# First-batch rows on two DMA queues, one 32-bit product for every second chunk, other first transfers by GpSimd

## The chip, the cores and the metric

The kernel runs on one NeuronCore of a Trainium2 chip. The metric is the device time of one launch in microseconds, smaller is better. TensorE (PE) multiplies, VectorE (DVE), ScalarE (ACT) and GpSimd (POOL) do the elementwise work, and SyncE (SP) issues DMA transfers; ACT and POOL can issue them too. Instructions of one engine run in the order in which the program lists them; between engines, semaphores make an instruction wait for the data it needs.

## The reference

Eight batches of 2496 rows of 256 numbers go through a Fourier mixing step and then through eight experts, of which each row uses one:

```python
X = np.fft.rfft(x, axis=1)                       # x: (8, 2496, 256)
Yr = X.real @ w_r - X.imag @ w_i + b_r
Yi = X.real @ w_i + X.imag @ w_r + b_i
Y = soft_threshold(Yr, 0.01) + 1j * soft_threshold(Yi, 0.01)
x = np.fft.irfft(Y, n=2496, axis=1).reshape(-1, 256)
e = argmax(x @ w_gate + modality_bias[modality_id])    # one of 8 experts
out = softmax_e * (relu(x @ w1[e]) @ w2[e])            # 256 -> 1024 -> 256
```

## The kernel before

The Fourier transform of length 2496 = 39 x 64 is done in two steps of matrix products. **Step 1** (`s1_*`) sums over 39 positions: rows of a batch lie in three groups of 39 partitions, 22 columns of 64 at a time, and a batch is 11 chunks of 512 numbers per partition. A chunk is split into a rounded high part (`x1h`) and a rest (`x1l`), and three products with the split constant `c_f` (L261 to L263) add up to the 32-bit result; ScalarE evicts it (L266). `s1_split` issues the split and, where rows are not there yet, their load; `s1_chunk` the products, the eviction and, for some chunks, the store to a scratch in DRAM (L277; for batch 0 after chunks 3, 7, 9 and 10, three transfers each, one per partition group).

**Step 2** (`a_load`, `s2_pair`) reads the scratch back in ten slabs of two frequencies (L286), so the first slab needs all stores of its batch, and multiplies by a quarter of table `c_m` in plain 32 bits (L295, one product of 128 columns shows as two instructions). `mix_bias` and `mix_sums` form the complex product with the split weights `wmix` (L332; 24 products of 256 columns for a slab), `shrink` is the threshold, `is2_pair` (L356, table `c_q`) and, at the end of a batch, `pivot` and `is1` are the inverse transform with the gate's product. `Route` then ranks the rows by expert and scatters them with indirect DMAs on GpSimd (L547); the expert stage follows after the eight batches.

The order on PE, ACT, DVE and POOL is the order of the program text (`manual_schedule`). `tc.issue_after(ins)` only keeps the transfers of its block behind `ins` on the same issuing queue. `build` writes the start out by hand (L1045 to L1088): constants and the rows of batch 0, eleven chunks of batch 0 with transfers of batch 1's rows and of table `m` between the stores, the mixing weights, the first slabs, then six chunks of batch 1 among the slab products `s2(0)`, `s2(1)`, the mixing `mix(0)` and its bias. The loop over batches and slabs (L1092 on) does for slab p of batch b: load slab p+4, product of slab p+2, chunks of batch 1 (while b is 0), mixing of slab p+1, inverse step of slab p. All plain transfers are issued by SP; GpSimd issues the scatters alone.

Each transfer has one of eight semaphores in turn; an issue waits until the transfer eight places before has landed.

Of the kernel before, what the change touches and what calls it, by code (L numbers as in the profile page):

```python
# [54 lines left out]
def shape_constants(nb):  # L55
# [39 lines left out]
    c_f = hl(cols(blk_f), 1).reshape(P1, 256)  # L95
    c_g = hl(cols(blk_g), 1).reshape(PK, 256)
# [12 lines left out]
    for c in range(2):  # L109
# [13 lines left out]
        "c_m": c_m, "c_q": c_q, "c_f": c_f, "c_g": c_g,  # L123
# [4 lines left out]
class Attn:  # L128
# [24 lines left out]
    def consts_first(self):  # L153

        nc, I, cp = self.nc, self.I, self.cp
        self.m = cp.tile([128, K1 * 128], F32, name="c_m")
        self.q = cp.tile([128, K1 * 128], F32, name="c_q")
        self.f = cp.tile([P1, 2, 128], F32R, name="c_f")
        st = self.w1.tile([128, 2, 256], F32, tag="u", name="st_f")[:P1].rearrange("p a b -> p (a b)")[:, :256]
        nc.sync.dma_start(st, I["c_f"])  # L160
        nc.vector.tensor_copy(self.f, st.rearrange("p (h k) -> p h k", h=2))
# [8 lines left out]
    def table_load(self, t, k):  # L170

        o = slice(k * 512, (k + 1) * 512)
        return self.nc.sync.dma_start((self.m if t == "m" else self.q)[:, o], self.I["c_" + t][:, o])

    def consts_mix(self):
        nc, I, cp = self.nc, self.I, self.cp
        st = []
        for i, nm in enumerate(("w_r", "w_i")):
            st.append(self.ww.tile([128, 520], F32, tag="wr", name=f"st_w{i}")[:, :512].rearrange("p (c d) -> p c d", c=2))
            nc.sync.dma_start(st[i], I[nm].rearrange("(c p) d -> p c d", p=128))  # L180
        for i, nm in enumerate(("b_r", "b_i")):
            nc.sync.dma_start(self.bias[64 * i:64 * i + 64, :],
# [28 lines left out]
    def s1_load(self, b, u, end=None, eng=None):  # L211
# [15 lines left out]
        for g in range(3):  # L227
            ins = eng.dma_start(xt[g * N1:(g + 1) * N1, :n, :], xv[:, GB[g] + 4 * u:GB[g] + 4 * u + n, :])
# [4 lines left out]
    def s1_split(self, b, c):  # L233
        nc = self.nc
        u, h = c // 2, c % 2
        for v in (u, u + 1):
# [5 lines left out]
        (nc.vector.tensor_copy if b == 1 or b == 0 and c % 2 == 0 else nc.scalar.copy)(xh, x)  # L242
# [3 lines left out]
    def s1_chunk(self, b, c, ahead):  # L246
# [3 lines left out]
        xh, xl = self.xs.pop((b, c))  # L250
# [10 lines left out]
        nc.tensor.matmul(ps[:PK], self.f[:, 0, :PK], xh, start=True, stop=False)  # L261
        nc.tensor.matmul(ps[:PK], self.f[:, 1, :PK], xh, start=False, stop=False)
        nc.tensor.matmul(ps[:PK], self.f[:, 0, :PK], xl, start=False, stop=True)  # L263
# [9 lines left out]
        if beg is not None:  # L273
            o = 0 if b == 0 else 4 * u
            for g in range(3):
                lo, hi = beg + (2 if g == 2 and beg == 0 else 0), 2 * c + 2
                self.stored = nc.sync.dma_start(  # L277
                    self.scr[b][:, GB[g] + lo:GB[g] + hi, :],
                    src[g * 2 * K1:(g + 1) * 2 * K1, lo - o:hi - o, :])

# [719 lines left out]
def build(tc, I, out, nb):  # L1000
    nc = tc.nc
    with ExitStack() as outer:
        dp = outer.enter_context(tc.tile_pool(name="wsp", bufs=1, space=DRAM))
        wsp = dp.tile([E * 128, 8192], F32, name="wsp")
        with ExitStack() as ctx:
# [40 lines left out]
            for u, v in ((0, 1), (1, 3), (3, 5)):  # L1046
                at.s1_load(0, u, v)
            first = at.s1_load(0, 5)
            at.s1_split(0, 0)
            at.s1_split(0, 1)  # L1050
            mixing = at.consts_mix()
            for c in range(11):
                at.s1_chunk(0, c, 2)
                with tc.issue_after(at.stored.ins if c > 2 else first.ins):
                    if c == 3:
                        at.table_load("m", 0)
                    elif c == 7:
                        at.s1_load(1, 0)
                    elif c == 9:
                        ins = at.s1_load(1, 1, 3)  # L1060
            with tc.issue_after(at.stored.ins):
                next(mixing, None)
                for i in range(3):
                    ins = load(i)
                    if i < 2:
                        with tc.issue_after(ins.ins):
                            ins = at.s1_load(1, 3, 5) if i else at.table_load("q", 0)
            with tc.issue_after(ins.ins):
                at.table_load("m", 1)
                rt.load_ids(0)  # L1070
            ahead1 = 6 if nb > 1 else 0
            at.s1_split(1, 0)
            at.s1_split(1, 1)
            for c in range(ahead1):
                with tc.issue_after(ins.ins):
                    at.s1_chunk(1, c, 2)
                if c == 1:
# [150 lines left out]
```

## Time and profile before

| | us |
|---|---|
| median of three runs | 1543.49 (1543.16 to 1543.94) |
| profiled execution | 1546.72 |
| its span, first to last instruction | 1544.9 |
| PE busy | 1497.0 (97%) |
| VectorE / ScalarE / GpSimd busy | 710.1 / 660.0 / 512.8 |

The profile is of one execution. PE runs are pipelined, so their ends are modelled. The granted clock of TensorE has two levels, 1.2 GHz (shown as 0.50) and 2.4 GHz (1.00).

### The profile page before, as it was taken

Reading aid. Unit: us, or ns where it says so; the run is one execution under the profiler, and the core shown is the slowest. Engines: PE = TensorE matmul, PEld = TensorE weight load, DVE = VectorE, ACT = ScalarE, POOL = GpSimd, SP = SyncE. Lnnn points to the kernel's source line nnn. Section 1 sums busy time; section 2 is a strip of 40 time slices with the busy share of each in tenths; the row PEclk is TensorE's granted clock in tenths of the full one; section 3 lists DMA queues with packets and bytes.
Section 4 is the critical chain, followed back from the end, with each engine's and each line's share of the span. In section 5 each row is a group of like instructions: output and inputs, shape, how many; then the busy total and the mean of one; then the engine's idle time right before and its main releaser. Section 6 shows DMA issues by size and latency. Waiting matters only on the chain. (4 is left out here: it accounts for less than half of the span.)

```text
span 1544.9 us, 35019 instructions
## 1 busy us (share of the span) xinstructions
PE 1497.0 (97%) x12459; PEld 1465.4 (95%) x12459; DVE 710.1 (46%) x1497; ACT 660.0 (43%) x1345; POOL 512.8 (33%) x511
## 2 busy tenths in 40 slices
PE   4899999999999999999999999999999999999998
PEld 2899999999999989999999999999999998999998
DVE  3676666666666665444333333333333333333332
ACT  2466766676757554523232332332323222233232
POOL 0001444444444545325532232322322323223232
PEclk8899999999999999999999999999999999999999
DMA  7857786868686666523443324552225238626440
GB/s 196 247 179 261 222 269 212 277 212 277 205 261 190 207 196 236 172 44 84 110 91 80 118 55 151 163 157 43 52 47 155 53 68 306 197 40 205 111 151 33
DMA packets 289589, 244.44 MB, mean 158 GB/s; under 512 B 208448, under 2 KB 243852, under 8 KB 285161
## 3 DMA queue, kind: packets, MB, share of 16 engines
q1 hardware_dynamic: 270421, 200.60, 44.9%
q0 software_dynamic: 18992, 41.58, 8.2%
q8 instruction: 100, 1.64, 0.5%
q14 instruction: 76, 0.62, 0.1%
HBM read 432.70 MB, written 100.08 MB: 345 GB/s over the span
## 5 line engine op out<-in xcount | busy, mean ns | idle before, releaser
L849 PE MATMUL y<-w,hh 128*128 128x256 f32 x2496 | 434.6, 278 | 0.2 <-DMA w<-wsp 0.2
L819 PE MATMUL h<-xh,w 128*128 128x256 f32 x2496 | 403.8, 278 | 4.1 <-DMA w<-wsp 4.1
L849 PEld LDWEIGHTS y<-w,hh 128*128 128x128 f32 x2496 | 377.8, 188 | 1.0 <-ACT xh L798 0.3
L849 PE MATMUL y<-w,hl 128*128 128x256 f32 x1248 | 347.2, 278 | 0.3 <-DVE hl L822 0.2
L819 PEld LDWEIGHTS h<-xh,w 128*128 128x128 f32 x2496 | 339.9, 189 | 4.5 <-issue 3.9
L822 DVE SCALAR_TENSOR_TENSOR hl<-h,hh 128x512 fp32r<-128x512 f32 x312 | 209.4, 689 | 232.2 <-ACT hh L821 188.5
L862 POOL DMA_INDIRECT out<-o,ix x161 | 158.5, 984 | 427.0 <-ACT o L841 389.7
L819 PE MATMUL h<-xl,w 128*128 128x256 f32 x1248 | 245.5, 278 | 0.0
L821 ACT ACTIVATE hh<-h 128x512 fp32r<-128x512 f32 x312 | 178.2, 595 | 155.7 <-PE h L819 137.0
L849 PEld LDWEIGHTS y<-w,hl 128*128 128x128 f32 x1248 | 234.3, 188 | 1.3 <-DVE hl L822 0.9
L819 PEld LDWEIGHTS h<-xl,w 128*128 128x128 f32 x1248 | 189.6, 189 | 0.0
L841 ACT ACTIVATE o<-y,xt 128x256 f32<-128x256 f32 x78 | 37.0, 475 | 343.0 <-PE y L849 343.0
L839 DVE TENSOR_SCALAR o<-y,xt 128x256 f32<-128x256 f32 x78 | 37.7, 484 | 314.2 <-ACT o L841 310.1
L332 PE MATMUL mx<-wmix,Xh 128*128 128x256 f32 x1280 | 180.7, 284 | 0.9 <-ACT mx L312 0.6
L799 POOL TENSOR_TENSOR xl<-tr,xh 128x512 fp32r<-128x512 f32 x78 | 101.0, 1295 | 192.9 <-ACT xh L798 192.9
L332 PEld LDWEIGHTS mx<-wmix,Xh 128*128 128x128 f32 x1280 | 160.6, 189 | 3.1 <-ACT mx L312 2.7
L547 POOL DMA_INDIRECT xs<-x1b,si x88 | 88.0, 1000 | 85.2 <-ACT ph L377 33.4
L372 PE MATMUL pv<-pv,z 128*120 128x136 f32 x704 | 111.0, 283 | 0.5 <-ACT z L359 0.5
L547 POOL DMA_INDIRECT xs<-x,si x88 | 87.9, 998 | 71.2 <-ACT ph L377 32.4
L994 POOL TENSOR_TENSOR wl<-wr,wh 128x512 fp32r<-128x512 f32 x46 | 58.5, 1273 | 148.2 <-ACT wh L993 133.7
L378 DVE TENSOR_TENSOR pl<-pv,ph 120x264 fp32r<-120x264 f32 x176 | 75.9, 431 | 68.4 <-ACT ph L377 58.2
L372 PEld LDWEIGHTS pv<-pv,z 128*120 128x120 f32 x704 | 99.5, 186 | 6.7 <-ACT z L359 0.7
(186 smaller groups left out, 1998.4 us busy)
## 6 DMA issues: line engine op xcount, KB each, us to landing
w<-wsp SPq DMA_DIRECT2D x166, 2048.0 KB
a<-scr SPq DMA_DIRECT2D x80, 256.0 KB
xt<-xs SPq DMA_DIRECT2D x624, 32.0 KB
wr<-in_moe_w SPq DMA_DIRECT2D x64, 256.0 KB
wsp<-wh SPq DMA_DIRECT2D x64, 256.0 KB
wsp<-wl SPq DMA_DIRECT2D x64, 256.0 KB
scr<-ev SPq DMA_DIRECT2D x98, 160.0 KB
x<-in_x SPq DMA_DIRECT2D x96, 156.0 KB
```

The costliest lines, as they stand in the source:

```text
L332: self.nc.tensor.matmul(ps[i][:, i, :], t[:, 2 * i + c, o:o + 128], self.w[:, wi, c, lo, :], start=False, stop=n == len(ops) - 1, skip_gro ...
L372: nc.tensor.matmul(ps[:PK, c * 128:c * 128 + D // 2 + E], self.z[:, o:o + 3, :, :].rearrange("p n k r -> p (n k r)"), self.pv[:, c, :], st ...
L378: nc.vector.tensor_sub(pl, ps[:PK, :GC], ph)
L547: i = self.nc.gpsimd.indirect_dma_start(out=self.xs, out_offset=bass.IndirectOffsetOnAxis(ap=si[:, k:k + 1], axis=0), in_=rows, in_offset= ...
L799: nc.gpsimd.tensor_sub(xl, tr, xh)
L819: nc.tensor.matmul(ps[:, q, :], w1[:, lo, c, f * 128:(f + 1) * 128], x[:, c, :], start=n == 0, stop=n == 5)
L821: nc.scalar.activation(hh[:, 2 * p:2 * p + 2, :], ps, AF.Relu)
L822: nc.vector.scalar_tensor_tensor(hl[:, 2 * p:2 * p + 2, :], ps, 0.0, hh[:, 2 * p:2 * p + 2, :], ALU.max, ALU.subtract)
L839: nc.vector.tensor_scalar_mul(o[:, s, :], y[s], gate)
L849: nc.tensor.matmul(y[s], lhsT, w2[:, lo, f, :], start=n == 0, stop=n == 23)
L862: ins = self.nc.gpsimd.indirect_dma_start(out=self.out, out_offset=bass.IndirectOffsetOnAxis(ap=ix, axis=0), in_=o, in_offset=None, bounds ...
L994: eng.tensor_sub(lo, raw, hi)
```

## The change

Rows of batch 0 for the third partition group are issued by ScalarE, those of the first two by SP. In batch 0 the even chunks are no longer split: one product of the plain 32-bit rows with the unrounded constant `c_f1` takes the place of three. The odd chunks are split on VectorE alone. Eight products of a zero tile in bf16 come first on PE and fourteen more after chunk 10. Of batch 0's stores the third group's goes by GpSimd, as do the mixing weights and biases (the generator `consts_mix` is first stepped after chunk 7, which issues its loads), batch 1's rows, most tables, and batch 2's rows. Four slabs are asked for directly behind the stores. Two chunks of batch 1 instead of six stand ahead of the loop, behind `s2(0)`, `s2(1)` and `mix(0)`; the rest follow two per slab. The routing constants and ids move to later slabs of batch 0.

```diff
 def consts_first(self):
+    self.blank = cp.tile([128, 512], BF16, name="blank")
+    nc.vector.memset(self.blank, 0.0)
+    self.f1 = cp.tile([P1, 128], F32, name="c_f1")
+    nc.sync.dma_start(self.f1, I["c_f1"])
...
+def consts_split(self):
+    st = ...
+    nc.scalar.dma_start(st, I["c_f"])
+    nc.vector.tensor_copy(self.f, st.rearrange("p (h k) -> p h k", h=2))
+
+def warm(self, n):
+    ps = self.ps.tile([128, 512], F32, tag="z", name=f"warm_{n}")
+    for _ in range(n):
+        self.nc.tensor.matmul(ps, self.blank[:, :128], self.blank, start=True, stop=True)
...
 # s1_load
         for g in range(3):
+            if b == 0:
+                eng = nc.scalar if g == 2 else nc.sync
...
 # s1_split
+        if b == 0 and h == 0:
+            return
...
-        (nc.vector.tensor_copy if b == 1 or b == 0 and c % 2 == 0 else nc.scalar.copy)(xh, x)
+        (nc.vector.tensor_copy if b < 2 else nc.scalar.copy)(xh, x)
...
 # s1_chunk
+        if b == 0 and h == 0:
+            nc.tensor.matmul(ps[:PK], self.f1[:, :PK], self.xt[b, u][:, :2, :].rearrange("p j d -> p (j d)"),
+                             start=True, stop=True)
+        else: (the three split products)
...
-                self.stored = nc.sync.dma_start(
+                ins = (nc.gpsimd if b == 0 and g == 2 else nc.sync).dma_start(
...
 # build, the start
             at.consts_first()
-            for u, v in ((0, 1), (1, 3), (3, 5)):
+            at.s1_load(0, 0)
+            at.consts_split()
+            for u, v in ((1, 3), (3, 5), (5, 6)):
                 at.s1_load(0, u, v)
-            first = at.s1_load(0, 5)
-            at.s1_split(0, 0)
+            ins = at.table_load("m", 0)
+            at.warm(8)
             at.s1_split(0, 1)
-            mixing = at.consts_mix()
+            mixing = at.consts_mix(nc.gpsimd)
             for c in range(11):
                 at.s1_chunk(0, c, 2)
-                (c == 3: table_load("m", 0); c == 7: s1_load(1, 0); c == 9: s1_load(1, 1, 3))
+                if c == 7:
+                    next(mixing, None)
             with tc.issue_after(at.stored.ins):
-                (mixing loads; load(0), table q, load(1), s1_load(1, 3, 5), load(2), table m, ids)
+                load(0)
+                ins = load(1)
             with tc.issue_after(ins.ins):
+                load(2)
+                ins = load(3)
+            for u, v in ((0, 1), (1, 2), (2, 3), (3, 5), (5, 6)):
+                at.s1_load(1, u, v, nc.gpsimd)
+                if u in (0, 2):
+                    at.table_load("q" if u == 0 else "m", u // 2, nc.gpsimd)
+            at.warm(14)
+            next(mixing, None)
+            s2(0)
+            bias(0)
+            s2(1)
             at.s1_split(1, 0)
             at.s1_split(1, 1)
+            mix(0)
+            bias(1)
+            ahead1 = 2
             for c in range(ahead1):
-                (six chunks, with s2(0), bias(0), s2(1), mix(0) between)
+                at.s1_chunk(1, c, 2)
...
 # build, slab p of batch 0
-                                    at.table_load("m", p // 2 + 2)
-                                at.table_load("q", p // 2 + 1)
+                                at.table_load("m", p // 2 + 2, nc.gpsimd)
+                            at.table_load("q", p // 2 + 1, nc.gpsimd)
...
-                        if p == 3:
+                        if p == 6:
                             late = [rt.consts(), at.consts_last()]
-                        if p in (3, 6):
+                        if p in (6, 8):
...
-                            at.s1_load(b + 2, (1, 2, 3, 5, 7, 9).index(p))
+                            at.s1_load(b + 2, (1, 2, 3, 5, 7, 9).index(p), None, None if b else nc.gpsimd)
```

## Rows read from the trace of the kernel before

**Rows 1.** Page of the profile, its first line and the first line of part 1: span; then for each engine busy us, share of the span and instructions (PE is TensorE's matmul, PEld its weight load, DVE VectorE, ACT ScalarE, POOL GpSimd).

```profile
span 1544.9 us, 35019 instructions
...
PE 1497.0 (97%) x12459; PEld 1465.4 (95%) x12459; DVE 710.1 (46%) x1497; ACT 660.0 (43%) x1345; POOL 512.8 (33%) x511
```

**Rows 2.** Windows of the execution. Columns: window, its length, then busy us (and instructions) of PE, PEld, DVE, ACT and POOL, the granted TensorE clock (1.00 is 2.4 GHz; before the first recorded change at 27 us the column shows 1.00 whatever the clock was), the mean busy share of the 16 DMA engines, and GB/s moved.

```profile
0.00:15.00 15.00, 5.41 (x12) 3.20 (x13) 4.85 (x10) 4.25 (x7) 0.19 (x4) 1.00 0.73 167
...
0.00:39.00 39.00, 15.70 (x39) 8.83 (x39) 12.60 (x25) 11.50 (x19) 0.19 (x4) 0.85 0.73 196
60.00:1540.00 1480.00, 1463.95 (x12317) 1441.08 (x12315) 682.98 (x1446) 639.86 (x1309) 512.51 (x507) 1.00 0.53 157
...
9.00:12.00 3.00, 0.60 (x2) 0.00 (x0) 0.00 (x0) 0.00 (x0) 0.00 (x0) 1.00 0.78 147
...
27.00:30.00 3.00, 0.00 (x0) 0.00 (x0) 0.00 (x0) 0.00 (x0) 0.00 (x0) 0.52 0.59 202
...
45.00:48.00 3.00, 2.99 (x12) 2.47 (x10) 2.48 (x6) 1.87 (x4) 0.00 (x0) 0.56 0.91 195
48.00:51.00 3.00, 2.24 (x15) 1.84 (x16) 2.93 (x6) 0.59 (x1) 0.00 (x0) 1.00 0.78 249
...
57.00:60.00 3.00, 3.00 (x30) 3.00 (x29) 2.44 (x6) 1.36 (x3) 0.00 (x0) 1.00 1.03 347
```

**Rows 3.** Waits of PE, longest in total first: before 50 us (first two rows) and from 60 us to the end (third row). Columns: who, line, released by whom, us in total, times, longest.

```profile
PE s L261 <- DVE x1h L242: 18.9, 4, 8.5
PE s L295 <- DMA a<-scr: 7.6, 1, 7.6
...
PE h L819 <- DMA w<-wsp: 4.1, 2, 3.7
```

**Rows 4.** Timeline of PE. Columns: start us, us, engine, line, operation, tiles and shapes, count merged into the row; in brackets the idle time before it and what ended it.

```profile
6.51 0.78 PE L261 MATMUL s<-x1h,c_f 117*120 117x512 f32 x1 [6.51 <-DVE x1h L242]
...
22.40 0.49 PE L263 MATMUL s<-x1l,c_f 117*120 117x512 f32 x1
...
41.89 2.05 PE L295 MATMUL s<-c_m,a 128*128 128x128 f32 x8 [7.57 <-DMA a<-scr]
...
46.29 1.69 PE L295 MATMUL s<-c_m,a 128*128 128x128 f32 x8
48.76 0.47 PE L261 MATMUL s<-x1h,c_f 117*120 117x512 f32 x1 [0.77 <-DVE x1h L242]
...
49.73 1.08 PE L332 MATMUL mx<-wmix,Xh 128*128 128x256 f32 x8
...
52.46 0.40 PE L261 MATMUL s<-x1h,c_f 117*120 117x512 f32 x1
...
53.18 1.06 PE L295 MATMUL s<-c_m,a 128*128 128x128 f32 x8
...
59.20 1.06 PE L295 MATMUL s<-c_m,a 128*128 128x128 f32 x8
60.01 0.48 PE L261 MATMUL s<-x1h,c_f 117*120 117x512 f32 x1
```

**Rows 5.** Timeline of SP's DMA queue: start of the issue, us the issue took (several merged where xN), line, tile written and tensor read.

```profile
0.74 0.47 SPq L160 DMA_DIRECT2D st_f<-in_c_f  x1
1.27 7.15 SPq L228 DMA_DIRECT2D x<-in_x  x12
...
23.08 4.35 SPq L228 DMA_DIRECT2D x<-in_x  x3
...
29.17 1.95 SPq L228 DMA_DIRECT2D x<-in_x  x3
31.23 1.04 SPq L277 DMA_DIRECT2D scr<-x1b  x3
...
39.02 0.37 SPq L286 DMA_DIRECT2D a<-scr  x1
```

**Rows 6.** Timeline of GpSimd (POOL) in the first batch's scatter: indirect transfers of 117 rows each.

```profile
177.98 0.99 POOL L547 DMA_INDIRECT xs<-x1b,si  x1 [1.38 <-ACT ph L377]
179.28 0.99 POOL L547 DMA_INDIRECT xs<-x1b,si  x1 [0.30 <-issue]
180.57 0.99 POOL L547 DMA_INDIRECT xs<-x1b,si  x1 [0.30 <-issue]
```

**Rows 7.** Timeline of VectorE and ScalarE: the first constant's use, the split of chunk 6 of batch 0, an eviction, and the split of batch 0's first slab product (which goes on with the half-size steps up to 45.73).

```profile
3.00 0.29 DVE L161 CAST c_f<-st_f 117x256 fp32r<-117x256 f32 x1 [3.00 <-DMA st_f<-in_c_f]
...
17.57 0.43 DVE L242 CAST x1h<-x 117x512 fp32r<-117x512 f32 x1 [1.40 <-PE s L262]
18.06 0.58 ACT L266 COPY x1b<-s 120x512 f32<-120x512 f32 x1
...
43.97 0.58 ACT L300 CAST Xh<-s 128x512 fp32r<-128x512 f32 x1 [9.03 <-PE s L295]
...
44.59 0.69 DVE L301 TENSOR_TENSOR Xl<-s,Xh 128x512 fp32r<-128x512 f32 x1 [3.77 <-ACT Xh L300]
45.73 0.42 DVE L303 TENSOR_TENSOR Xl<-Xh,s 128x256 fp32r<-128x256 f32 x1 [0.45 <-ACT Xh L302]
```

More of the change, by code (lines that the diff above doesn't have):

```diff
@@ L95, in shape_constants @@
     c_f = hl(cols(blk_f), 1).reshape(P1, 256)
+    c_f1 = np.ascontiguousarray(cols(blk_f), np.float32)
     c_g = hl(cols(blk_g), 1).reshape(PK, 256)
@@ L122, in shape_constants @@
         "c_tri": tri, "c_grid": grid(seg), "c_grid2": grid(seg, seg, np.zeros((3, 1)), half),
-        "c_m": c_m, "c_q": c_q, "c_f": c_f, "c_g": c_g,
+        "c_m": c_m, "c_q": c_q, "c_f": c_f, "c_f1": c_f1, "c_g": c_g,
         "c_tok": np.concatenate([tok, valid], 1),
@@ L260, in s1_chunk @@
         ps = pool.tile([128, 512], F32, tag=tag, name=f"s1_{b}_{c}")
[L261 to L263 removed]
+        if b == 0 and h == 0:
+            nc.tensor.matmul(ps[:PK], self.f1[:, :PK], self.xt[b, u][:, :2, :].rearrange("p j d -> p (j d)"),
+                             start=True, stop=True)
+        else:
+            xh, xl = self.xs.pop((b, c))
+            nc.tensor.matmul(ps[:PK], self.f[:, 0, :PK], xh, start=True, stop=False)
+            nc.tensor.matmul(ps[:PK], self.f[:, 1, :PK], xh, start=False, stop=False)
+            nc.tensor.matmul(ps[:PK], self.f[:, 0, :PK], xl, start=False, stop=True)
         if ahead and c + ahead < 11:
@@ L1053, in build @@
                 at.s1_chunk(0, c, 2)
[L1054 to L1060, printed above, removed]
-            with tc.issue_after(at.stored.ins):
[L1062 to L1067, printed above, removed]
@@ L1072, in build @@
+            at.warm(14)
[3 more added lines that the diff above has]
+            s2(1)
             at.s1_split(1, 0)
             at.s1_split(1, 1)
+            mix(0)
+            bias(1)
+            ahead1 = 2
             for c in range(ahead1):
-                with tc.issue_after(ins.ins):
-                    at.s1_chunk(1, c, 2)
-                if c == 1:
-                    s2(0)
-                    next(mixing, None)
-                    bias(0)
-                if c == 3:
-                    s2(1)
@@ L1083, in build @@
-                if c == 4:
-                    mix(0)
-            bias(1)
-            ins = load(3)
-            with tc.issue_after(ins.ins):
-                at.s1_load(1, 5)
+                at.s1_chunk(1, c, 2)
             state = None
@@ L1107, in build @@
                         if p == 9:
-                            sw.load()
-                            sw.load()
-                        if p == 3:
+                            with tc.issue_after(ins.ins):
+                                sw.load()
+                                sw.load()
+                        if p == 6:
                             late = [rt.consts(), at.consts_last()]
-                        if p in (3, 6):
+                        if p in (6, 8):
                             with tc.issue_after(ins.ins):
@@ L1120, in build @@
                         ahead(i)
-                    if p == 1 and b > 0:
-                        rt.load_ids(b)
+                    if p == 1:
+                        with tc.issue_after(ins.ins):
+                            rt.load_ids(b)
                     if p in (1, 2, 3, 5, 7, 9) and b + 2 < nb:
                         with tc.issue_after(ins.ins):
-                            at.s1_load(b + 2, (1, 2, 3, 5, 7, 9).index(p))
+                            at.s1_load(b + 2, (1, 2, 3, 5, 7, 9).index(p), None, None if b else nc.gpsimd)
                     if b > 0 and p < (7 if b < 5 else 6):
```

24 lines of the change are left out of this document (10 added, 14 removed).

## The prediction

> **What bounds the kernel now.** I read the page first: TensorE (PE) is busy 97% of 1544.9 us, the next engine 46% [rows 1]. So only two things can shorten the program: less PE work, or less time in which PE has nothing to do. The windows say where PE is idle: 1463.95 of the 1480 us from 60 to 1540 are busy, but 15.70 of the first 39 [rows 2]. The waits agree: 27 us before 50 us are waits for first-batch rows and for the first slab of the scratch, and after 60 us the longest single wait is 3.7 us [rows 3]. From the mixing product at 49.73 on PE runs practically without a gap, so what the change does to that point it does to the end, one for one.
>
> What sets 49.73 is read from the PE timeline and SP's queue side by side. Chunk 6 of batch 0 can start only at 17.57, when its rows are split [rows 7]; the eleven chunks end at 22.40 + 0.49 [rows 4]. Their results go to the scratch, but SP puts six transfers of batch 1's rows (1.4 MB) between the stores: issues at 23.08 and 29.17, the last stores at 31.23, and the first slab is asked for only at 39.02, when all stores have landed [rows 5]. It is there at 41.89 [rows 4]. PE has then been idle for 19 us, save two chunks of batch 1, and runs at the lower of its two clock levels: the granted clock is 0.52 in 27 to 30 and 0.56 in 45 to 48, so it fell at about 27.1 (4.2 us after the last product) and rose at about 47.6, 5.7 us after work resumed [rows 2, 4].
>
> **The change part by part.** Everything before the first mixing product is re-laid; I follow the chain to it.
>
> *Rows of batch 0.* 2.57 MB go as before, a third of them now by ScalarE's queue, plus 0.06 MB for c_f1. Later end: the rate does not move, chunk 6 starts 0.06 MB / 0.167 MB per us = 0.4 us later, 17.9. Earlier end: the 2.34 MB of rows that chunk 6 needs, with 0.18 MB of constants, move at the 0.347 MB per us of 57 to 60 instead of the 0.167 of the first 15 us [rows 2]: 7.3 us from 2, so 9.3. I take 15.5, nearer to the row of the same transfers, yet below it, because 0.147 in 9 to 12, with nothing but these rows under way [rows 2], is less than half of what the same queue moves later.
>
> The Trainium skill speaks against this step. "DMA: Bandwidth & Descriptors", section "Issuing engines are not separate DMA queues", says that transfers of all issuing engines run on the same 16 DMA engines, and that a second issuer saves issue time only. SP's twelve issues took 7.15 us from 1.27, long before 17.57 [rows 5, 7], so by that rule nothing is saved here; that is a rival below.
>
> *32-bit products.* The six even chunks lose a cast and a subtraction on VectorE and three products, and get one 32-bit product. A product of four slabs, 4 x 128 columns in 32 bits, takes 0.81 us (59.20 to 60.01); three split products of 512 columns take 0.72 (52.46 to 53.18) [rows 4]. So PE pays 0.1 us more per even chunk at full clock (6 x 0.1), all inside its idle time; if the clock is low, 1.7 [rows 4] for 0.81. In exchange chunks 6 and 7 need 0.81 + 0.72 + an eviction of 0.58 [rows 7] and some 0.4 of hand-over: chunk 7 is out at 15.5 + 2.5 = 18.0; call it T. At low clock T is 1.5 later.
>
> *Zero products.* 8 before the first rows, 14 after chunk 10. PE waits there anyway (until 6.51 [rows 4] and, from 20, for the slab), so their 3 us each cost nothing. The first eight may make the chunks run at full clock. The fourteen end near 24; the slab comes more than 4.2 us later by the sum below, so I let the clock fall as it did at 27.1 and count no gain; if the cover were gone, 14 products cost 14 x 0.24 = 3.4 us.
>
> *Transfers by GpSimd.* Its queue gets, in this order from T: a third of the store of chunks 4 to 7, the four of the mixing weights and biases (they are asked for at chunk 7, not at the start), the thirds of the last two stores, then fifteen of batch 1's rows with two tables between them. The trace has no plain transfer on this queue. Below: SP's 0.37 us per issue (39.02). Above: an indirect one occupies it 0.99 us and follows the last by 1.29 us [rows 5, 6]. I take P = 1.1, nearest to GpSimd's own row, since most have 39 or 40 rows instead of 117. So the last store is written out at T + 7P = 25.7 and landed 2.3 us later (the first constant, 0.74 to 3.00 [rows 5, 7]): the slab is asked for at 28.0 instead of 39.02. Check by bytes: constants 0.18, rows 2.57, table 0.26, stores 2.56, weights and biases 0.65 = 6.2 MB must move before; from 1.5 on that ends at 19.4 by the rate of 57 to 60 and at 33.2 by the 0.196 of the first 39 us [rows 2]. 28.0 lies between; both ends are kept.
>
> *From the slab to the mixing product.* Arrival 2.9 us after the request (39.02 to 41.89): 30.9. Two slab products at low clock, 1.7 each [rows 4], then the split of the first, 43.97 to 46.15 on ScalarE and VectorE, begins 0.5 after its products [rows 7]: 30.9 + 1.7 + 0.5 + 2.2 = 35.3 for the mixing product, against 49.73. The clock rises 5.7 us after 30.9, at 36.6, so 1.3 us of the mixing run at half speed and lose 0.7. Five chunks of batch 1 that PE had done by 49.73 are now still to do: 5 x 0.72 = 3.6. Shift: 35.3 + 0.7 + 3.6 - 49.73 = -10.1.
>
> *What is late next.* The third slab product needs the second quarter of table m, eleventh on GpSimd's queue after the stores: T + 18P + 2.3 = 40.1; PE is there at 35.3 + 0.7 + 2.7 + 1.4 = 40.1. No cover is left, so I charge one wait of the size of 48.76's, 0.77 [rows 4]: -9.4. Constants and ids moved to later steps of batch 0, its later tables and batch 2's rows on GpSimd: used 9 us or more after issue, since a step of that loop takes 6 us (53.18 to 59.20 [rows 4]); PE covers them, and I cost them at nothing; if one is late, it costs a wait like the 3.7 of [rows 3].
>
> *Sum.* The profiled execution took 1546.7 us around a span of 1544.9; minus 9.4 gives 1537.3 around 1535.5. The timed runs' median, 1543.5, lies 3.2 below that execution: 1534.1, say 1534.0.
>
> **The rivals.**
> 1. *The second queue brings the rows nothing.* Chunk 6 at 17.9, T and all behind it 2.4 later: 1536.4. For it: SP's issues are far ahead of use. Against: the low rate while only rows move.
> 2. *Bytes bind, not issue.* The store lands at 33.2 by the old mean rate: 5.2 later, 1539.2. For it: less than 28 us for 6.2 MB needs a rate that only later windows show.
> 3. *Both relieved.* Rows at the 0.249 MB per us of 48 to 51 [rows 2], so chunk 6 at 12.1 and T at 14.6, GpSimd's issue near SP's 0.37, and all 6.2 MB at 0.28, between 0.249 and 0.347: stores landed at 23.6 instead of 28.0, so 4.4 earlier throughout: 1529.6. For it: nothing holds a queue of its own but bytes. Against: no row shows two queues at once.
> 4. *Slower: GpSimd's issue becomes the bound.* It must write seventeen transfers before batch 1's rows and both tables are out, which SP did at 0.4 us each. The third slab product stood at 53.18 before; with four more chunks to do behind it, 4 x 0.72, it may come at 50.3 for no change. T + 18P + 2.3 reaches that at P = 1.67; at P = 2.0 it is 56.3 and the time 1549.5. Between 1.5 and 1.83 nothing is to be measured. For it: 128 rows of a table or 256 of a weight may take longer than 117 of a scatter. Against: the scatter's 1.29 holds the reading of its indices too. For it also speaks the same page, section "SWDGE vs HWDGE vs iDMA": GpSimd writes its descriptors into SBUF, from which VectorE locks it out in some modes. The scatters' 0.99 us stand beside a VectorE 46% busy [rows 1, 6], so the trace shows no such loss.
>
> **How the numbers follow.** Forecast 0.41, rival 1 0.20, rival 2 0.13, rival 3 0.11, no measurable change (P 1.5 to 1.83) 0.08, slower 0.07. A measurement tells 0.2%, 3.1 us, from no change. Faster: 0.41 + 0.20 + 0.13 + 0.11 = 0.85; same 0.08; slower 0.07. The forecast's own range, P from 0.9 to 1.3 and T from 16.5 to 19.5, is 1531 to 1538. The range for 8 in 10 reaches to rival 3 and past rival 2: 1528 to 1540.5.
>
> **What would show it.** Right: the request for the first slab near 28, the first mixing product near 35, PE without gaps from there, and GpSimd's transfers about 1.1 us apart. Chunk 6 starting at 17 to 18 speaks for rival 1; GpSimd idle while the stores land late, for rival 2; that request before 25, for rival 3; PE waiting for table m or rows of batch 1 after 38, for rival 4. The prediction is wrong if the first mixing product comes after 46, or if it comes early and PE loses it again before 100 us.

## The result, and the profile after

The changed kernel takes 1554.86 us (median of six runs, 1552.54 to 1561.44), the kernel before 1543.33 us in the same session (1542.34 to 1544.77). The ratio is 1.0083, interval 1.0060 to 1.0107: slower by 0.8%, where 9.4 us less were forecast. The profiled execution took 1556.07 us around a span of 1554.3, 9.4 us more than the span before. The medians lie 11.5 us apart; what follows takes apart the 9.4 of the two profiled executions. First the page: span, engines and DMA queues (packets, MB, share of 16 engines' span).

```profile
span 1554.3 us, 35059 instructions
...
PE 1503.1 (97%) x12475; PEld 1466.2 (94%) x12475; DVE 706.3 (45%) x1491; ACT 657.3 (42%) x1340; POOL 540.4 (35%) x561
...
q1 hardware_dynamic: 266453, 190.55, 42.3%
q0 software_dynamic: 22192, 50.69, 10.3%
...
q10 hardware_dynamic: 338, 1.00, 0.3%
```

PE has 6.1 us more busy time than in [rows 1]. GpSimd has 50 instructions more, all of them plain transfers; q0 is its queue, q10 ScalarE's and q1 SP's. The windows, with the columns of [rows 2]:

```profile
0.00:33.00 33.00, 20.66 (x49) 8.88 (x49) 7.46 (x16) 7.72 (x12) 6.82 (x16) 0.96 0.72 193
0.00:39.00 39.00, 20.66 (x49) 8.88 (x49) 8.17 (x17) 7.72 (x12) 11.75 (x25) 0.89 0.74 202
39.00:60.00 21.00, 13.09 (x67) 11.58 (x68) 7.76 (x15) 5.72 (x12) 7.43 (x15) 0.64 0.96 245
60.00:1540.00 1480.00, 1464.62 (x12321) 1441.21 (x12320) 689.24 (x1459) 643.43 (x1316) 519.23 (x520) 1.00 0.53 156
```

From 60 us on PE is as busy as before (1464.62 of 1480 us, 1463.95 in [rows 2]), so the loss lies ahead of 60 us or behind the last product. PE's waits up to 90 us name the place:

```profile
PE s L317 <- DMA a<-scr: 19.4, 2, 15.6
```

The wait for the slabs of the scratch has grown from 7.6 us [rows 3] to 19.4. The timeline of PE:

```profile
1.19 3.59 PE L180 MATMUL warm<-blank 128*128 128x512 bf16 x8 [1.19 <-DVE nlam L167]
7.29 2.03 PE L277 MATMUL s<-x,c_f 117*120 117x512 f32 x2 [2.51 <-DMA x<-in_x]
...
13.74 2.06 PE L277 MATMUL s<-x,c_f 117*120 117x512 f32 x2 [3.13 <-DMA x<-in_x]
...
19.85 1.02 PE L277 MATMUL s<-x,c_f 117*120 117x512 f32 x2
...
43.06 2.05 PE L317 MATMUL s<-c_m,a 128*128 128x128 f32 x8 [15.57 <-DMA a<-scr]
48.96 2.07 PE L317 MATMUL s<-c_m,a 128*128 128x128 f32 x8 [3.85 <-DMA a<-scr]
50.68 2.05 PE L354 MATMUL mx<-wmix,Xh 128*128 128x256 f32 x8
...
55.04 0.40 PE L281 MATMUL s<-x1h,c_f 117*120 117x512 f32 x1
...
56.45 1.05 PE L317 MATMUL s<-c_m,a 128*128 128x128 f32 x8
```

s2(0) starts 1.2 us later than before (41.89 in [rows 4]), although the chunks are through at about 24.4 and the zero products at 27.5. s2(1), which had its slab in time before, waits another 3.9 us. The first mixing product comes at 50.68 instead of 49.73. The mixing takes 4.36 us to the chunk at 55.04 (2.73 from 49.73 to 52.46 in [rows 4]), as its first products still run at the lower clock level: 1.63 more. Then there are five chunks of batch 1 to do that had been done, 5 x 0.72 = 3.6. Sum: 0.95 + 1.63 + 3.6 = 6.2 us. Product for product, PE is 6.3 us late at 78 us and 6.4 us late at the end.

Why the slabs are late is read from SP's queue and GpSimd's, side by side. SP's:

```profile
1.25 9.44 SPq L242 DMA_DIRECT2D x<-in_x  x8
...
17.72 13.09 SPq L297 DMA_DIRECT2D scr<-x1b  x8
36.28 15.14 SPq L308 DMA_DIRECT2D a<-scr  x6
```

GpSimd's:

```profile
22.58 0.55 POOL L297 DMA_DIRECT2D scr<-x1b  x1 [3.78 <-ACT x1b L286]
23.11 0.78 POOL L192 DMA_DIRECT2D st_w<-in_w_r  x1
...
25.67 1.08 POOL L297 DMA_DIRECT2D scr<-x1b  x2
26.69 0.55 POOL L242 DMA_DIRECT2D x<-in_x  x1
29.84 0.52 POOL L242 DMA_DIRECT2D x<-in_x  x1 [2.59 <-DMA scr<-x1b]
...
32.85 0.56 POOL L185 DMA_DIRECT2D c_q<-in_c_q  x1 [0.59 <-DMA st_w<-in_w_i]
33.41 2.50 POOL L242 DMA_DIRECT2D x<-in_x  x5
```

SP has its last store of batch 0 written out at 30.81 (17.72 + 13.09), GpSimd its last at 26.75 (25.67 + 1.08). Yet the first slab is asked for at 36.28: the last stores took 5.5 us from there to land. In the meantime GpSimd had gone on at once to what stood next in its queue, batch 1's rows and the tables; nothing holds these back but its own eight places (one of the rows waited 2.59 us for a store of GpSimd's, at 29.84). How much of the DMA engines each queue had is shown by the queues in the window from 24 to 48 us, of the changed kernel:

```profile
q0 software_dynamic: 1360, 4.15, 63.4%
q1 hardware_dynamic: 1123, 1.72, 25.7%
```

and of the kernel before:

```profile
q1 hardware_dynamic: 2387, 5.35, 79.3%
```

SP's queue, with two thirds of the stores and all slabs, was left with a quarter of the DMA engines' time; GpSimd's had 63%, most of it for rows and tables that nobody needed before 50 us.

The remaining 3 us are behind the last product. The start of the last scatter, in the changed kernel and in the kernel before:

```profile
1545.50 0.97 POOL L884 DMA_INDIRECT out<-o,ix  x1 [1.76 <-DVE o L861]
```

```profile
1539.14 0.97 POOL L862 DMA_INDIRECT out<-o,ix  x1 [1.76 <-DVE o L839]
```

From there to the end of the span are 8.8 us (1554.3 - 1545.50) against 5.8 (1544.9 - 1539.14). Most of that time is GpSimd's closing drain instruction, 5.71 us against 3.26 in the trace's records, which is 2.45 of the 3.0; it also starts 0.6 us later behind the scatter. 6.4 + 3.0 = 9.4 us of span.

### The profile page after: what moved, and what is told of

It reads as the page before. It is cut to its first block, busy times and chain, and to the rows that moved or that the text cites. A ratio compares the mean times of both kernels' runs of the same rounds, so it can differ in the third digit from the quotient of the medians.

```text
span 1554.3 us, 35059 instructions
## 1 busy us (share of the span) xinstructions
PE 1503.1 (97%) x12475; PEld 1466.2 (94%) x12475; DVE 706.3 (45%) x1491; ACT 657.3 (42%) x1340; POOL 540.4 (35%) x561
## 3 DMA queue, kind: packets, MB, share of 16 engines
q0 software_dynamic: 22192, 50.69, 10.3%
## 5 line engine op out<-in xcount | busy, mean ns | idle before, releaser
L569 POOL DMA_INDIRECT xs<-x1b,si x88 | 88.0, 1000 | 84.5 <-ACT ph L399 35.3
```

The lines of the kernel that those rows point to most:

```text
L569: i = self.nc.gpsimd.indirect_dma_start(out=self.xs, out_offset=bass.IndirectOffsetOnAxis(ap=si[:, k:k + 1], axis=0), in_=rows, in_offset= ...
```

## The experiments

The theory: what GpSimd issues, held back by nothing, shares the DMA engines with batch 0's last stores and the first slabs. The rivals: bytes at a fixed rate bind, whoever issues them; the weights, asked for at chunk 7, are what stands in the way; GpSimd's plain transfers cost at the end of the program alone; the zero products matter. Experiments go by their labels, e1 to e16. The first four stand beside a kernel before of 1544.38 us.

**Batch 1's rows back on SP, behind the four slabs.**

```diff
-            for u, v in ((0, 1), (1, 2), (2, 3), (3, 5), (5, 6)):
-                at.s1_load(1, u, v, nc.gpsimd)   # and tables q0, m1 by nc.gpsimd
+            with tc.issue_after(ins.ins):
+                for u, v in ((0, 1), (1, 2), (2, 3), (3, 5), (5, 6)):
+                    at.s1_load(1, u, v)          # and the tables, on SP
```

> Batch 1's rows and the two tables among them go back to SP's queue, behind the four slabs; all else as in the changed kernel. Theory 'turns' (slab reads lose because GpSimd's queue has large transfers under way on the same DMA engines): the stores stop competing with batch 1's rows, the first slab is asked for at 32 to 34 instead of 36.3, arrives about 3 us later instead of 6.6, slabs 1 to 3 follow about 1 us apart instead of 4 to 6, the first mixing product comes at 39 to 42 instead of 50.7, and the time falls by 6 to 11 us against the changed kernel. Rival 'bytes' (the same bytes must move, whoever issues them): the slabs come early but PE then waits for batch 1's rows or table m, which now stand behind them, and the time stays within 3 us of the changed kernel.

Measured (e1): 1552.87 us, ratio 1.0065 (1.0041 to 1.0089). The slabs did land close together, so that s2(0) and s2(1) ran back to back, but the request was no earlier (37.13). Its GpSimd timeline shows what took their place: the rows gone, GpSimd ran ahead to what came next in its queue, the tables of the loop (26.03, 28.48) and batch 2's rows (from 30.84). The time stayed within 3 us of the changed kernel's, as the rival had it; that the request would be no earlier was expected by neither. Taking away one load put another in its place, so e1 alone could not tell the theory from bytes.

**The weights asked for at the start, no zero products, and batch 2's rows on GpSimd in the kernel before.**

```diff
             mixing = at.consts_mix(nc.gpsimd)
+            next(mixing, None)
             for c in range(11):
                 at.s1_chunk(0, c, 2)
-                if c == 7:
-                    next(mixing, None)
```

> The mixing weights and biases are asked for at the start, not after chunk 7. If the stores land late because these 0.65 MB stand among them on GpSimd's queue and on the engines, the first slab is asked for some 3 us earlier (0.65 MB at the 0.21 MB per us of that stretch), and the time falls by about 3 us. Rival: at the start they delay the rows of batch 0 by as much, chunk 7 comes 2 to 3 us later, and the time stays within 1 us.

Measured (e2): 1559.2 us, ratio 1.0096 (1.0076 to 1.0116). The request moved from 36.28 to 39.17 and s2(0) from 43.06 to 51.20. 0.65 MB put ahead of the stores made the request 2.9 us later; at the 0.2 MB per us of the first 39 us they take 3.2. So asking early gains nothing; that it costs this much neither side had expected.

```diff
-            at.warm(8)
-            at.warm(14)
```

> The changed kernel without its 8 + 14 zero products. If they do nothing: clock up at about 20 us as before, the first slab asked for within 0.5 us of 36.3, time within 1 us. If the eight warm the clock for the first chunks: chunks 2 to 5 later, clock up 2 to 4 us later, time 1 to 3 us longer. If the fourteen cost PE: time shorter by up to 3 us.

Measured (e4): 1555.66 us, ratio 1.0061 (1.0042 to 1.0080); request at 34.96, s2(0) at 42.89, mixing at 51.21. The interval overlaps with the changed kernel's: the zero products cost or gain nothing that can be told here.

```diff
-                            at.s1_load(b + 2, (1, 2, 3, 5, 7, 9).index(p))
+                            at.s1_load(b + 2, (1, 2, 3, 5, 7, 9).index(p), None, None if b else nc.gpsimd)
```

> The kernel before, with batch 2's rows (18 transfers) alone issued by GpSimd. Theory 'drain' (the more plain transfers GpSimd has issued, the longer it drains at the very end): the start up to 60 us is as before, GpSimd's last drain is longer than the 3.3 us of before, 4.2 if in proportion to the number of transfers or 5.7 if any suffice, and the time is 1 to 3 us over the kernel before. Rival (the drain's length has to do with the last outputs): the drain is 3 to 3.6 us and the time that of the kernel before within 1 us.

Measured (e3): 1551.43 us, ratio 1.0042 (1.0028 to 1.0056), 7 us over the kernel before where 1 to 3 were expected. This edit of the kernel before was meant to touch the end alone, and touched the start. GpSimd's timeline:

```profile
1.30 1.83 POOL L228 DMA_DIRECT2D x<-in_x  x3 [0.86 <-POOLq L1218]
```

Batch 2's first rows, which stand in slab 1 of the loop, go out at 1.30 us, beside batch 0's: the first chunk starts at 8.97 instead of 6.51 [rows 4], and s2(0) 3.0 us later. At the end, the last scatter to the end of the span takes 6.8 us instead of 5.8. One edit, two costs: a transfer that runs ahead, and a longer end.

**What is left when GpSimd has no plain transfers behind its stores, or none.** The next four stand beside a kernel before of 1544.35 us.

```diff
# the first run's edit, and in the loop
-                            (tables and batch 2's rows) ..., nc.gpsimd)
+                            with tc.issue_after(ins.ins): (the same on SP)
```

> The changed kernel, but GpSimd keeps only the third group's four stores and the weights and biases; batch 1's rows and the first tables are asked for by SP behind the four slabs, the loop's tables and batch 2's rows by SP as in the kernel before. The theory (transfers that GpSimd issues with nothing to hold them back share the DMA engines with the last stores and the first slabs) expects the first slab to be asked for at 31 to 33 us instead of 36 to 37, to land 3 to 4 us later, the first mixing product at 37 to 40 us instead of 50.7, GpSimd's last drain near 3.5 us instead of 5.7, and a time of 1534 to 1541 us. The rival (the bytes of the start bind, whoever issues them) expects the request at 35 us or later, mixing at 46 us or later, and 1547 to 1553 us.

Measured (e7): 1547.3 us, ratio 1.0016 (1.0003 to 1.0029). Request at 34.27, s2(0) at 37.24, s2(1) right behind it, mixing at 41.59, 9.1 us before the changed kernel's and 8.1 before [rows 4]. The theory's numbers for the start are missed by less than 2 us, but its time (1534 to 1541) by 6; the time is the rival's, the start is not. s2(2) waits 3.5 us in this trace, and e8 shows for what.

```diff
# on top of the run above
-            mixing = at.consts_mix(nc.gpsimd)
+            mixing = at.consts_mix(nc.sync)
...
-                ins = (nc.gpsimd if b == 0 and g == 2 else nc.sync).dma_start(
+                ins = nc.sync.dma_start(
```

> The run above with the third group's stores and the weights on SP too, so that GpSimd issues no plain transfer at all. What is left of the change: ScalarE's row queue, the 32-bit products, the zero products, the slabs directly behind the stores, two chunks ahead of the loop. The theory expects within 3 us of the run above (a third of the stores shares SP's queue again, 0.5 us an issue) and the last drain at 3.3 us as in the kernel before; if the stores that GpSimd issues are slow in themselves, this run is faster by 2 us or more. The rival (bytes) expects no difference and 1547 us or more.

Measured (e8): 1544.66 us, ratio 0.9999 (0.9990 to 1.0009). SP's queue and PE's timeline:

```profile
32.52 1.92 SPq L308 DMA_DIRECT2D a<-scr  x4
...
36.18 4.54 SPq L242 DMA_DIRECT2D x<-in_x  x6
41.18 0.36 SPq L185 DMA_DIRECT2D c_m<-in_c_m  x1
...
35.55 3.76 PE L317 MATMUL s<-c_m,a 128*128 128x128 f32 x16 [8.90 <-DMA a<-scr]
39.91 1.19 PE L354 MATMUL mx<-wmix,Xh 128*128 128x256 f32 x8 [0.60 <-ACT mx L334]
...
49.17 2.04 PE L317 MATMUL s<-c_m,a 128*128 128x128 f32 x8 [4.54 <-DMA c_m<-in_c_m]
```

It is 2.6 us faster than e7: GpSimd's own four stores and the weights cost as well, 1.75 us at the request and 0.7 at the end, though the weights also go out some 11 us earlier here, so that the stores' part in it is not told apart. The theory was right about the slab and wrong about the time. Request at 32.52, s2(0) at 35.55, mixing at 39.91, 9.8 us before the kernel before. But then s2(2) waits 4.5 us at 49.17 for the second quarter of c_m, asked for at 41.18, behind nine transfers of rows. Ahead of the loop only two chunks of batch 1 stand ready to fill such a gap, and s2(2)'s 2.04 us show the lower clock level once more. Five chunks still to do take 3.6 of the 9.8; this wait and the clock take the rest.

```diff
# on top of e8
-            if b == 0:
-                eng = nc.scalar if g == 2 else nc.sync
```

> The run above with all rows of batch 0 on SP's queue. If two queues bring batch 0's rows no sooner (the rows landed at 17.8 us in the changed kernel, 18.0 us in the one before), the time is within 1.5 us of the run above; if the second queue helps, chunk 10 starts later by 1 us or more and the time is longer by as much.

Measured (e9): 1544.96 us, ratio 1.0003 (0.9989 to 1.0017). No difference in time; in its one profile s2(0) starts at 37.80, 2.2 us later, with chunk 6 at 19.22 (18.86 in e8). The rows are not what differs most: with twelve rows ahead of them on SP's queue, the weights are issued up to 21.29 us there (14.56 in e8), and the first store behind three of them at 19.16 (16.72).

```diff
# on top of e8
-        if b == 0 and h == 0:      # in s1_split: no split of even chunks
-            return
```

(and the three split products for all chunks of batch 0)

> The run without plain GpSimd transfers, with all chunks of batch 0 split and multiplied in three products instead of every second one in one 32-bit product. If the rows' landing sets when the last store goes out, the time is within 1 us of that run; if the split of the even chunks was on the path, the last chunk of batch 0 starts later by 1 to 2 us and so does all that follows.

Measured (e10): 1544.94 us, ratio 0.9998 (0.9988 to 1.0007), s2(0) at 35.54 against 35.55. The 32-bit products gain nothing: the rows' landing and the stores' way set the slab.

**Mending the new wait; the fourth corner; the end alone.** Beside a kernel before of 1545.96 us.

```diff
# on top of e8
                 load(0)
                 ins = load(1)
             with tc.issue_after(ins.ins):
-                load(2)
-                ins = load(3)
-            (rows 0, q0, rows 1, rows 2, m1, rows 3 to 5 of batch 1)
+                at.s1_load(1, 0, 1)
+                at.table_load("m", 1)
+                ins = load(2)
+            (q0, slab 3, then the other rows of batch 1)
```

> The run without plain GpSimd transfers, with the second quarter of table c_m and the first rows of batch 1 asked for ahead of the third slab, instead of the table behind all rows of batch 1. The theory (in that run the 9.8 us that the first mixing product came earlier were given back because s2(2) waited 4.5 us for c_m, with two chunks ready ahead of it and not six, after which the clock was at its lower level once more) expects no wait of s2(2) over 1 us, the clock full from about 41 us on, and 4 to 6.5 us less: 1538 to 1541 us, faster than the kernel before. The rival (what is won at the start is given back later by something that paces the loop, whatever comes first) expects another wait at 45 to 60 us, for rows or a slab, and 1543 to 1546 us again.

Measured (e11): 1542.29 us, ratio 0.9976 (0.9959 to 0.9993): faster than the kernel before. SP, PE and windows:

```profile
32.21 0.90 SPq L308 DMA_DIRECT2D a<-scr  x2
...
34.44 0.36 SPq L185 DMA_DIRECT2D c_m<-in_c_m  x1
...
34.91 3.60 PE L317 MATMUL s<-c_m,a 128*128 128x128 f32 x16 [8.43 <-DMA a<-scr]
39.26 1.18 PE L354 MATMUL mx<-wmix,Xh 128*128 128x256 f32 x8 [0.75 <-ACT mx L334]
...
43.83 1.05 PE L317 MATMUL s<-c_m,a 128*128 128x128 f32 x8
...
0.00:33.00 33.00, 19.09 (x49) 8.17 (x49) 8.14 (x17) 7.73 (x12) 0.19 (x4) 0.82 0.68 193
39.00:60.00 21.00, 20.29 (x141) 17.55 (x142) 15.66 (x30) 10.60 (x22) 0.00 (x0) 1.00 0.83 234
```

s2(2) follows the chunks without a wait, the clock is 1.00 from 39 to 60 us, and PE is busy for 20.29 of these 21 us (13.09 in the changed kernel). The rival, something that paces the loop whatever comes first, falls: no such wait shows. The gain is smaller than was expected, 3.7 us by the medians for 4 to 6.5, and 1542.29 lies above 1538 to 1541; the one profile's span is 5.5 us shorter than the kernel before's. In the first 33 us the DMA engines move 193 GB/s here and in the changed kernel alike: what differs is which bytes.

```diff
# on top of e11
-                if c == 7:
-                    next(mixing, None)
...
             with tc.issue_after(ins.ins):   # behind slab 1
+                next(mixing, None)
                 at.s1_load(1, 0, 1)
```

> The run above with the mixing weights and biases asked for behind the second slab instead of ahead of the last two groups of stores. If bytes ahead of the last store set when the first slab is asked for, the request comes 1.5 to 2.5 us sooner (32.5 us in the run without plain GpSimd transfers) and the first mixing product as much, less what the weights' split on VectorE now waits for; the time is 1 to 2 us below the run above. If the issue of the stores, one by one behind eight semaphores, sets it, the request moves by less than 1 us and the time is that of the run above, or longer where mixing waits for the weights.

Measured (e12): 1545.55 us, ratio 0.9990 (0.9980 to 1.0000). The request came 0.8 us sooner (31.43), not 1.5 to 2.5, and the later weights and rows cost more than that. PE:

```profile
40.13 2.08 PE L354 MATMUL mx<-wmix,Xh 128*128 128x256 f32 x8 [2.15 <-ACT mx L334]
...
49.14 0.46 PE L281 MATMUL s<-x1h,c_f 117*120 117x512 f32 x1 [2.14 <-DVE x1h L258]
```

Mixing had to wait 2.2 us, and the third chunk of batch 1 2.1 us for its rows. The 0.65 MB do not shift the last store as e2 led me to expect: from 27 to 37 us the queues had 78% of the DMA engines' time in the changed kernel, 56% in e11, so here bytes are not all that binds. SP's last store is written out at 28.94, 0.8 us sooner than in e11; what paces SP's stores was not found.

```diff
# the changed kernel; of the edits of e7 only those in the loop
```

> The changed kernel with the loop's tables and batch 2's rows back on SP, held behind the slabs, while GpSimd keeps its stores, the weights, batch 1's rows and the first two tables: the fourth corner beside the changed kernel, the run with batch 1's rows on SP and the run with both on SP. The theory expects that what GpSimd issues next, whatever it is, shares the DMA engines with the last stores and the slabs: first slab asked for at 34 to 37 us and landed 5 us or more later, mixing at 47 us or later, 1548 to 1553 us. If only the loop's transfers did harm, it is near the run with both on SP: request at 34 to 35 us, landed within 3.5 us, 1546 to 1549 us.

Measured (e14): 1557.58 us, ratio 1.0062 (1.0037 to 1.0086). PE's slab products:

```profile
41.76 2.05 PE L317 MATMUL s<-c_m,a 128*128 128x128 f32 x8 [15.37 <-DMA a<-scr]
47.07 2.08 PE L317 MATMUL s<-c_m,a 128*128 128x128 f32 x8 [3.27 <-DMA a<-scr]
```

With batch 1's rows alone on GpSimd the start is the changed kernel's again: request at 35.16, landed 6.6 us later, and s2(1) waits for its slab. The start is what the theory expected, the time lies above its 1548 to 1553 us. So of the four corners (both on GpSimd 1.0083, loop's tables and batch 2's rows alone 1.0065, batch 1's rows alone 1.0062, neither 1.0016) either load is enough. Whichever GpSimd issues next does the harm. No run kept these transfers on GpSimd and held them behind the slabs; that they harm by going early, and not by standing on GpSimd's queue, is argued and not shown. For it speaks the kernel before: there SP's own rows and weights stood about the last stores, which were written out by 32.27 and had landed only at 39.02 [rows 5], against 2.5 us in e8 and e11.

```diff
-                            at.s1_load(b + 2, (1, 2, 3, 5, 7, 9).index(p))
+                            at.s1_load(b + 2, (1, 2, 3, 5, 7, 9).index(p), None, nc.gpsimd if b in (2, 3) else None)
```

> The kernel before, with the rows of batches 4 and 5 (36 plain transfers) issued by GpSimd, so that nothing of the start is touched. The theory (GpSimd's wait at the end of the program grows with the number of its plain transfers: 3.3 us with none, 3.9 with 18, 5.1 with 33, 5.7 with 50) expects no shift of PE's instructions over 0.5 us at 60 us and the span to end 7.8 to 8.5 us behind the start of the last indirect scatter, 5.8 us in the kernel before: some 2 to 2.5 us longer. The rival (the longer end comes from the late start and what it moves) expects 5.8 us and the time of the kernel before.

Measured (e13): 1553.57 us, ratio 1.0047 (1.0032 to 1.0062). The start is untouched (PE is 0.6 us early at 60 us). The last scatter:

```profile
1544.12 0.97 POOL L862 DMA_INDIRECT out<-o,ix  x1 [1.76 <-DVE o L839]
```

From there to the end of the span, 1551.8, are 7.7 us, just under what was expected and far from the rival's 5.8. The other 5 us came ahead of that scatter, which neither side foresaw: PE falls 3.2 us back between 166 and 313 us, while GpSimd issues these rows (from 208 us on). PE's waits in that stretch name mixing, which waits for ScalarE's `mx`, 0.3 us in two waits in the kernel before:

```profile
PE mx L332 <- ACT mx L312: 3.3, 5, 1.2
```

Why ScalarE is late there was not followed further.

**The order with little else.** Most of what was left of the change in the version that is faster was taken out: no second row queue, all chunks split, no zero products; then the zero products alone put back. The order of SP's transfers stays, with two chunks ahead of the loop in place of six, constants and ids later in batch 0, and the odd chunks' cast on VectorE. Beside a kernel before of 1535.01 us.

```diff
# on top of e11; and as in e10 all chunks split
-            if b == 0:
-                eng = nc.scalar if g == 2 else nc.sync
...
-            at.warm(8)      # second run: kept
-            at.warm(14)     # second run: kept
```

> The run with the table ahead of the third slab, with what else the change brought taken out: batch 0's rows all on SP, all chunks split and multiplied in three products, no zero products. What is left is the order of the transfers on SP's queue and two chunks ahead of the loop in place of six. If the order alone carries the gain (two queues brought the rows no sooner, the 32-bit products moved no store), the first slab product starts at 35 to 38 us and the time is within 2 us of that run and 0.15 to 0.35 % below the kernel before. If the rows' second queue or the 32-bit products carry a part, the first slab product starts at 38 us or later and the time is that of the kernel before or longer.

> The run above with the twenty-two zero products back. If they raise TensorE's clock for the chunks and that shortens the way to the last store, the first slab product starts 1 us or more sooner than in the run above and the time is as much less; if the rows' landing sets the chunks, as the run of the changed kernel without zero products showed where other things were late, both start within 0.5 us and the times are the same.

Measured (e15, e16): 1530.01 us, ratio 0.9973 (0.9962 to 0.9984), and 1531.52 us, ratio 0.9978 (0.9965 to 0.9990). The first of the two, SP and PE:

```profile
33.28 0.89 SPq L304 DMA_DIRECT2D a<-scr  x2
...
36.19 3.76 PE L313 MATMUL s<-c_m,a 128*128 128x128 f32 x16 [12.19 <-DMA a<-scr]
40.55 2.08 PE L350 MATMUL mx<-wmix,Xh 128*128 128x256 f32 x8 [0.60 <-ACT mx L330]
```

s2(0) starts at 36.19 (36.48 with the zero products): about 1 us later than with all parts (34.91 in e11, 35.55 in e8). What is left carries the gain: the order of SP's transfers and the two chunks ahead of the loop, which were not tried apart. The second queue, the 32-bit products and the zero products carry none that can be measured.

## Why the prediction was wrong

*The step that failed: "the last store is written out at T + 7P = 25.7 and landed 2.3 us later", the slab asked for at 28.0.* Both terms failed. T + 7P follows GpSimd's queue and puts SP's stores at nothing. GpSimd's last store was out at 26.75, near the forecast, but SP's at 30.81. Its last five stand in 8.20 us, and the last seven in 7.39 in e11, which has no plain GpSimd transfer (SP's queue from 23 to 31 us, the changed kernel first, then e11):

```profile
22.61 8.20 SPq L297 DMA_DIRECT2D scr<-x1b  x5
```

```profile
22.32 7.39 SPq L297 DMA_DIRECT2D scr<-x1b  x7
```

Of these, SP waited 0.6 and 0.2 us for a chunk's result; the rest is 1.5 and 1.0 us a store, where the kernel before wrote its last three in 1.04 us [rows 5]. Then the landing took 5.5 us (30.81 to 36.28) and not 2.3. The 2.3 came from the first constant, alone on the engines [rows 5, 7], though [rows 5] had the stores themselves: out at 32.27, the slab asked for at 39.02, 6.8 us later.

From there the slab took 6.8 us to arrive (36.28 to 43.06) and not 2.9, and mixing came 7.6 us behind it and not 4.4, since s2(1) stands ahead of it on PE and waited for its own slab. Mixing at 50.68 instead of 35.3 is thus 5.1 (SP's last store) + 3.2 (landing) + 3.9 (arrival) + 3.2 (s2(1)) = 15.4 us late; it is also past the 46 us that the prediction gave as its sign of being wrong. With 0.9 more at the low clock, 3.0 at the end, and 0.8 charged for a wait that did not come, that makes 18.5 of the 18.8 us between the 9.4 forecast as gain and the 9.4 measured as loss.

e11 tells the two failures apart. Without plain GpSimd transfers SP's last store is out at 29.72, the landing takes 2.5 us, the arrival 2.7 and mixing comes 4.35 behind it: only the first term is still off, by 4.0 us, and the other 10.3 us are gone. These I had priced at nothing: each transfer moved to GpSimd was priced by when its data is used, and not by what it takes from transfers under way. GpSimd's queue moved 4.15 MB from 24 to 48 us, SP's with the stores and slabs 1.72 (5.35 in the kernel before). e8 (landing 2.5, arrival 3.0) and e14 (6.8 and 6.6) show the same two sides. Why SP's stores are issued slowly with and without GpSimd's transfers stays open.

The Trainium skill's section "Queues, rings and completion order" ("DMA: Bandwidth & Descriptors") says that each DMA engine takes the queues that have work in turn, a packet at a time. No view used here shows single packets in turn, but the shares fit: in that window a packet of SP's queue has 1.5 KB and one of GpSimd's 3.1, the packets are 1123 and 1360, and SP's queue had 26% of the time against 63%.

*Rivals 1 and 2.* Chunk 6 was to start at 15.5; it started at 19.85. The 17.57 of [rows 7], from which that was reckoned, was no landing: its bracket names PE. Where VectorE did wait for these rows, they were there at 17.24 in e13, whose start is that of the kernel before, and at 17.21 here, for chunk 7's split:

```profile
17.21 0.43 DVE L258 CAST x1h<-x 117x512 fp32r<-117x512 f32 x1 [1.27 <-DMA x<-in_x]
```

So rival 1 was right, the rows land when they did. The Trainium skill's section "Issuing engines are not separate DMA queues" ("DMA: Bandwidth & Descriptors") had the answer, and I gave it 0.20. The rest, to 19.85, is chunks 2 to 5 at the lower clock level, at which a 32-bit product shows 2.06 us. Rival 2 had 33.2 for a term that I set at 28.0; without plain GpSimd transfers the slab is asked for at 32.5, 32.2 and 33.3 (e8, e11, e15), and its gain of 4.3 us (1543.5 to 1539.2) is near e11's 3.7. That the size fits is partly luck: taking 0.65 MB out of the way moved the request by 0.8 us (e12), not by the 3 that bytes at that rate would give.

*32-bit and zero products.* Both cost nothing, as said, and gain nothing: e10 and e4. The first eight go with a higher clock for chunk 0 in some runs (1.09 us in e8's profile), not in the changed kernel (2.03 at 7.29), and where it does, it is gone by 13 us.

*GpSimd's issue.* P was taken as 1.1 us from the scatters; a plain transfer takes 0.51 to 0.59, the first store and the weights 0.73 to 0.79. Mis-sized by half, yet GpSimd's last store was out at 26.75 instead of 25.7, since T was 22.6 and not 18.0: two errors that nearly cancel, by luck.

*From the slab on.* The rest of the sum held: with what was measured for mixing and for the low clock, 50.68 + 1.63 + 3.6 - 49.73 = 6.2, against the 6.3 of the trace. The loss to the low clock was 1.6 and not 0.7. The third slab product did not wait in the changed kernel, as everything ahead of it was late; where that was mended it waited 4.5 us (e8) rather than 0.77, behind SP's rows, not GpSimd's issue.

*Transfers in the loop "cost at nothing".* Wrong twice: they are asked for early (e1, e3), and each GpSimd transfer is paid for at the end of the program, 3.0 us for fifty. No step had this.

*Rival 4* had the sign and not the cause: GpSimd's issue was never late, it was too early.

## What to carry to other kernels

A transfer moved to an idle queue also loses what held it back. And when one queue's share is moved away, time what is left on the other, too. Price it by the transfers that will then be under way beside it, above all those that the next stage waits for, not by its issue time or by when its data is used. When a critical load has been brought forward, look through the same queue for the next table behind it: here the first mixing product came 9.8 us earlier and the time was the same, until one table stood ahead of six of the row transfers.

## What the runs showed of the hardware that was not expected

- *GpSimd's end.* From the last scatter's start to the end of the span, by the number of plain transfers that GpSimd had issued in the whole program:

```
plain transfers   0     8     18    25    33    36    50
us              5.7-5.8 6.4   6.8   7.5   8.1   7.7   8.8
run        before,e8,e11,e15 e7 e3  e14   e1   e13   after
```

  It grows by some 0.06 us a transfer, not strictly by their number (33 and 36); what the engine does in that time was not looked into.
- *One rate.* In the first 33 us the DMA engines moved 189 to 203 GB/s in the kernel before, the changed one and all runs but e12, whichever queue asked; they were busy for 0.67 to 0.76 of that time. e12, which asks for the weights later, moved 174.
- *The clock's return.* After PE took up work again with s2(0), full speed came back at about 38 in e11 (3 us later), 44 in e15 (8) and 54 in the changed kernel (11, with a gap between): one row of the trace before, 5.7 us, was no price for it.
